# A mixture-of-experts kernel: products of the two widest experts split in three, a cast moved to ScalarE, and the order of h's halves changed

## The chip, the core and the metric

The kernel runs on one core of a Trainium2 chip, as one program. The metric is device time in microseconds; the kernel before takes 565.54 us (median of 3 runs, 563.86 to 566.18). The engines are named as in the profile: PE (TensorE) for matrix products, DVE (VectorE), ACT (ScalarE), POOL (GpSimd), and SP, whose queue issues most transfers. Times of the trace are us from the start of the span.

## What is computed

Attention with a threshold, then a layer that sends each of 1152 tokens to one of eight experts, then a SwiGLU layer, all in float32. The part that matters here is the middle one:

```python
logits = x @ w_gate                      # x: 1152 x 512, 8 experts
expert_idx = np.argmax(logits, axis=1)
# token i goes into its expert's rows, at most `capacity` (288) of them
h = np.maximum(np.einsum('ecd,edf->ecf', disp, w1), 0.0)   # 512 -> 1024
y = np.einsum('ecf,efd->ecd', h, w2)                       # 1024 -> 512
out[i] = gate_w[i] * y[expert_idx[i], pos[i]]
# and behind it
silu(out @ w_gate2) * (out @ w_val) @ w_out                # 512 -> 1536 -> 512
```

## The kernel before

**Precision.** Every operand of a product is kept as two parts, a rounded one (hi) and the rest (lo), and a product is made as hi x hi + hi x lo + lo x hi. What the text calls a *split* is the making of the two: a cast gives hi, a subtraction gives lo.

**Stages.** Attention is followed by a router that sorts the tokens by expert and the experts by how many tokens they have. `rest` then runs the experts in order of rank, fewest tokens first, with a fixed width of token columns for each rank: the list `FAST` (L56) is 128, 128, 128, 144, 176, 192, 224, 224. Other lists stand in two other branches, which don't run with these inputs. Ranks 0 to 2 run in another form (`expert_rows`). Ranks 3 to 7 run in `expert`, on which the change bears. In the trace rank 3 begins at 232.47 us, rank 4 at 249.81, rank 5 at 269.13, rank 6 at 288.73 and rank 7 at 309.68; the gate products (L1471, then L1460) begin at 332.02.

**One expert of width W.** Its token columns are taken out of `xsT` by `window` (L1219): DVE casts them into the hi half of `xw` (L1226) and subtracts for the lo half (L1227). That is done for rank e+1 just behind the first tile of rank e's second product (for rank 3 inside `expert_rows` of rank 2). The *first product* makes h in eight steps f = 0 to 7, each into a tile `ps_h` of PSUM: per step four pairs of matmuls, one of hi weights with hi and lo columns side by side (2W columns, L1231) and one of lo weights with the hi columns (W columns, L1232). The two column halves of the result are then added by `total` (L1236): ACT copies one half into `a` (L1240), DVE adds the other (L1241, the *sum*). `finish` (L1356) makes the split of h: ACT applies relu (L1357, hi), DVE makes the *remainder* (L1358, lo). `finish` of step f-1 is called at step f, after `total` of f. The *second product* makes y in four tiles m = 0 to 3, each over all eight h, with eight pairs; `total` adds the halves, ACT casts into `yT` (L1405) and DVE subtracts (L1406).

**Weights.** They come as raw pieces of 1 MB by DMA from SP's queue. Each piece is split by ACT (cast, L210) and DVE (L288). `next_piece` issues ACT's cast at once and keeps DVE's subtraction back until it is called the next time. In the first product it is called after every odd step, in the second after every tile. In rank 7 `pump` puts the decoding of the gate weights (64-bit values to float32, L231 to L238, on ACT and DVE) between the steps.

**Order.** In this part PE, ACT, DVE and POOL run in the order in which the code is written, each engine through its own queue. Nothing is reordered: an operation that waits holds up all behind it on its engine.

Of the kernel before, what the change touches and what calls it, by code (L numbers as in the profile page):

```python
# [22 lines left out]
def attention_moe_swiglu_kernel(  # L23
# [15 lines left out]
    nc = tc.nc  # L39
    B, H, S, D = q.shape  # L40
    NT, DM = out.shape
# [200 lines left out]
    def enqueue(it):  # L242
        while late:
            late.pop()()
        for x in range(NCV):
            if (it, x) not in converted:
                converted.add((it, x))
                queue.extend((it, op) for op in convert_ops(it, x))

    def pump(n=1):  # L250
        for _ in range(min(n, len(queue))):
            queue.popleft()[1]()
# [715 lines left out]
    V = nc.vector  # L968
# [53 lines left out]
    with nc.allow_low_precision("counts of at most 9 are exact in bfloat16"):  # L1022
        V.tensor_reduce(out=osb[:, 0:B],
                        in_=oh[:, 0:B * C4].rearrange("p (b t) e -> p b e t", b=B),
# [110 lines left out]
    def rest(ctx, WS, drops):  # L1135
# [33 lines left out]
        xsT = mx.tile([128, KD, YW], F32, name="xsT")  # L1169
# [3 lines left out]
        offs_v, offs_a = {0: 0}, {0: 0}  # L1173
# [5 lines left out]
        def sort_scale(t):  # L1179
            if t < NTL:  # L1180
                V.tensor_scalar(out=grow[t][:, 0:DM], in0=grow[t][:, 0:DM],
                                scalar1=grow[t][:, DM:DM + 1], scalar2=None, op0=ALU.mult)
# [14 lines left out]
        def mm3(o, wp, ws, x, xs, first, last):  # L1197
            mm(o, ws(wp, 0), xs(x, 0), start=first, stop=False)
            mm(o, ws(wp, 0), xs(x, 1), start=False, stop=False)
            mm(o, ws(wp, 1), xs(x, 0), start=False, stop=last)  # L1200
# [13 lines left out]
            ev()  # L1214
        sort_scale(NS0)
        sort_scale(NS0 + 1)
        V.memset(xsT[:, :, NT:], 0.0)

        def window(e):  # L1219
            offs_v[e] = ldv(e, EDVE)  # L1220
            offs_a[e] = ldv(e, EACT)
            xw = xws[e] = mw.tile([128, KD, 2 * WIN], F32R, tag="xw", name="xw")
            W = WS[e]
            assert steps["t"] * 128 >= (NT if drops else min(NT, sum(WS[:e + 1])))
            src = xsT[:, :, bass.ds(offs_v[e], W)]
            V.tensor_copy(out=xw[:, :, 0:W], in_=src)  # L1226
            V.tensor_tensor(out=xw[:, :, W:2 * W], in0=src, in1=f32(xw[:, :, 0:W]), op=ALU.subtract)  # L1227

        def mm_win(W, ps, wp, ws, x, first, last):
            if 2 * W <= 512:  # L1230
                mm(ps[:, 0:2 * W], ws(wp, 0), x[:, 0:2 * W], start=first, stop=False)  # L1231
                mm(ps[:, 0:W], ws(wp, 1), x[:, 0:W], start=False, stop=last)  # L1232
            else:
                mm3(ps[:, 0:W], wp, ws, x, lambda x, i: x[:, i * W:(i + 1) * W], first, last)

        def total(W, ps):  # L1236
            if 2 * W > 512:
                return ps[:, 0:W]
            a = sm.tile([128, WIN], F32, tag="a", name="a")[:, 0:W]
            nc.scalar.copy(a, ps[:, W:2 * W])  # L1240
            V.tensor_tensor(out=a, in0=a, in1=ps[:, 0:W], op=ALU.add)  # L1241
            return a
# [3 lines left out]
        def sort_step():  # L1246
            n, t = steps["n"], steps["t"]
            steps["n"] += 1
            for _ in range(1 if drops else SORT[n] if n < len(SORT) else 0):
                if t < NTL:  # L1250
                    sort_tile(t)()
                    sort_scale(t + 2)
                    if t == NG0 - 1:
                        idle.append(gbuf)
                        next_raw()
                    t += 1
            steps["t"] = t
# [86 lines left out]
        def flush_tail():  # L1344
            while tails:
                f, a = tails.pop()
                f(*a)

        def expert(e):
            if e < NE - 1 and WS[e] == 128:  # L1350
                return expert_rows(e)
            xw = xws.pop(e)
            W = WS[e]
            hs = []

            def finish(h, a):  # L1356
                nc.scalar.activation(out=h[:, 0:W], in_=a, func=ACTF.Relu)  # L1357
                V.scalar_tensor_tensor(out=h[:, W:2 * W], in0=a, scalar=0.0, in1=f32(h[:, 0:W]),  # L1358
                                       op0=ALU.max, op1=ALU.subtract)

            for f in range(KF):
                if f % 2 == 0:
                    wp = pieces.pop(("w1", e, f // 2))
                wv = wp[:, :, :].rearrange("p i (k f) -> p i k f", k=KD)
                ps = ps8.tile([128, 512], F32, tag="m", name="ps_h")
                fo = (f % 2) * 128
                for kk in range(KD):
                    mm_win(W, ps, wv, lambda w, i: w[:, i, kk, fo:fo + 128], xw[:, kk],
                           kk == 0, kk == KD - 1)
                flush_tail()  # L1370
                h = hp_.tile([128, 2 * WIN], F32R, tag="h", name="h")
                a = total(W, ps)
                if f:
                    finish(*prev)
                prev = h, a
                if f == KF - 1:
                    finish(*prev)
                hs.append(h)
                sort_step()
                if e == NE - 1:  # L1380
                    if f == CV:
                        enqueue(porder[npm])
                    pump(PU[f])
                for _ in range((EP if e and WS[e] < EW else (0, 1, 0, 1, 0, 1, 0, 1))[f]):
                    if used["piece"] < npm:
                        next_piece()
            for m in range(KD):
                ps = ps8.tile([128, 512], F32, tag="m", name="ps_y")
                if e in halves:
                    for f in range(KF):  # L1390
                        wv = pieces["w2", e, f // KD * 2 + m // 2][:, :, :].rearrange(
                            "p i (k f) -> p i k f", k=KD)
                        mm_win(W, ps, wv, lambda w, i: w[:, i, f % KD, m % 2 * 128:m % 2 * 128 + 128],
                               hs[f], f == 0, f == KF - 1)
                else:
                    wp = pieces.pop(("w2", e, m))
                    wv = wp[:, :, :].rearrange("p i (k f) -> p i k f", k=KF)
                    for f in range(KF):
                        mm_win(W, ps, wv, lambda w, i: w[:, i, f], hs[f], f == 0, f == KF - 1)
                if e == 0:  # L1400
                    sl_a = sl_v = slice(0, W)
                else:
                    sl_a, sl_v = bass.ds(offs_a[e], W), bass.ds(offs_v[e], W)
                a = total(W, ps)
                nc.scalar.copy(yT[:, 0, m, sl_a], a)  # L1405
                V.tensor_tensor(out=yT[:, 1, m, sl_v], in0=a, in1=f32(yT[:, 0, m, sl_v]),  # L1406
                                op=ALU.subtract)
                if e in halves and e < NE - 1:
                    for _ in range((0, 1, 0, 3)[m]):
                        next_piece()  # L1410
                elif e < NE - 1:
                    next_piece()
                else:
                    if m == MG[0]:
                        next_piece()
                    if m == MG[1]:
                        enqueue(porder[npm + 1])
                    pump(PU[KF + m])
                    if m == KD - 1:
                        next_piece()  # L1420
                if m == 0 and e + 1 < NE:
                    window(e + 1)

        for e in range(NE):
            expert(e)
            if e == SE:
                nc.scalar.activation(out=warm, in_=warm, func=ACTF.Silu)
# [89 lines left out]
    with tc.If(nmx <= NT, preferred_fallthrough_block=True) as cmp:  # L1517
        with ExitStack() as arm:
            rest(arm, FAST, False)
    with cmp.Else():  # L1520
        nmw = nc.values_load(slack[0:1, 1:2], min_val=0, max_val=2 * NT)
        with tc.If(nmw <= NT) as cmw:
            with ExitStack() as arm:
                rest(arm, WIDE, False)
        with cmw.Else():
            with ExitStack() as arm:
                rest(arm, SAFE, True)
# [29 lines left out]
```

## Time and profile before

| | |
|---|---|
| median of 3 runs | 565.54 us (563.86 to 566.18) |
| profiled execution | 564.97 us, its span 563.3 us |
| mean granted clock of PE | 0.986 |
| PE busy | 536.4 us (95% of the span) |
| DVE busy | 409.7 us (73%) |
| ACT busy | 295.2 us (52%) |
| POOL busy | 85.4 us (15%) |
| ranks 3 to 7 | 232.47 to 332.02 us |

The profile's page gives busy time for the whole span; the tables of stretches give it for one part. "Busy" of PE is a modelled time, since matmuls are pipelined: how long a matmul really takes of PE is read from the distance between the starts of two. An operation on DVE or ACT starts a little before the one in front ends. In a row of the timeline the bracket at the end is the idle time of the engine before that operation, and what ended it.

### The profile page before, as it was taken

What the parts mean: (1) busy time and instruction counts of PE and PEld (TensorE: products, weight loads), DVE (VectorE), ACT (ScalarE), POOL (GpSimd) and SP (SyncE); (2) the same over time, 40 slices, a digit from 0 to 9 for tenths busy, and PEclk for the clock granted to TensorE, in tenths of its full rate; (3) what the DMA queues carried; (4) which work ended last, traced back from release to release, by engine and by line L of the source; (5) the groups of instructions that cost most, each with busy time, mean ns of one, the idle gap of its engine ahead of it and who ended that gap; (6) DMA issues with size and microseconds to landing.
All of it is one profiled execution on the core that took longest, in us unless ns stands there. A gap on an engine that the chain in (4) does not pass through costs nothing. (4 is left out here: it accounts for less than half of the span.)

```text
span 563.3 us, 9844 instructions
## 1 busy us (share of the span) xinstructions
PE 536.4 (95%) x3600; PEld 481.0 (85%) x3602; DVE 409.7 (73%) x825; ACT 295.2 (52%) x573; POOL 85.4 (15%) x145
## 2 busy tenths in 40 slices
PE   7999988999997799999999999999999999999996
PEld 6787866877773799998998889999999999888884
DVE  5988876888876399989988977888896748722220
ACT  4977664676651399877866743334332333332321
POOL 6541050055452500000000000000000000011101
PEclk8999998999999799999999999999999999999999
DMA  7557467457301888977666442442341300000001
GB/s 185 173 150 171 118 143 172 110 140 205 116 29 35 313 289 281 328 224 232 224 219 223 151 149 81 145 149 83 143 149 76 112 40 1 0 38 37 20 38 42
DMA packets 67895, 77.94 MB, mean 138 GB/s; under 512 B 25216, under 2 KB 43136, under 8 KB 67840
## 3 DMA queue, kind: packets, MB, share of 16 engines
q1 hardware_dynamic: 66256, 72.52, 42.4%
q0 software_dynamic: 1440, 4.72, 2.2%
q8 instruction: 30, 0.49, 0.3%
q14 instruction: 25, 0.20, 0.1%
q10 hardware_dynamic: 144, 0.00, 0.0%
HBM read 61.89 MB, written 4.72 MB: 118 GB/s over the span
## 5 line engine op out<-in xcount | busy, mean ns | idle before, releaser
L1460 PE MATMUL pgv<-yT,ring 128*128 128x384 f32 x828 | 145.1, 337 | 0.0
L1460 PEld LDWEIGHTS pgv<-yT,ring 128*128 128x128 f32 x828 | 144.9, 188 | 0.0
L210 ACT CAST ring<-raw 128x1024 fp32r<-128x1024 f32 x57 | 60.8, 1066 | 51.2 <-DVE raw L238 49.5
L657 ACT COPY pT<-ps_pt 128x512 f32<-128x512 f32 (+1 forms) x108 | 52.3, 486 | 41.6 <-PE ps_pt L653 41.6
L607 DVE TENSOR_REDUCE nm<-s 128x1 f32<-128x576 f32 x72 | 54.4, 755 | 17.2 <-PE s L597 17.1
L631 DVE SCALAR_TENSOR_TENSOR e<-s,th,e 128x576 f32<-128x576 f32 x72 | 58.7, 816 | 6.2 <-ACT e L620 4.9
L1513 POOL DMA_INDIRECT out_dram<-ob,ids x9 | 8.7, 972 | 358.9 <-ACT ob L1512 351.7
L620 ACT ACTIVATE e<-s,nm 128x576 f32<-128x576 f32 x72 | 54.3, 754 | 2.2 <-DVE nm L607 1.8
L288 DVE TENSOR_TENSOR ring<-raw,ring 128x1024 fp32r<-128x1024 f32 x44 | 53.3, 1218 | 0.0
L1231 PE MATMUL ps_y<-h,ring 128*128 128x448 f32 (+3 forms) x160 | 48.8, 370 | 3.6 <-DVE h L1358 3.4
L214 DVE TENSOR_TENSOR hs<-h,hs 128x768 fp32r<-128x768 f32 x18 | 17.2, 958 | 48.1 <-ACT hs L210 48.1
L653 PE MATMUL ps_pt<-ident,e 128*128 128x128 f32 x324 | 47.9, 276 | 0.0
L1231 PE MATMUL ps_h<-xw,ring 128*128 128x448 f32 (+3 forms) x160 | 46.4, 362 | 0.0
L1508 PE MATMUL po<-ring,hs 128*128 128x512 f32 x108 | 42.0, 389 | 0.0
L1507 PE MATMUL po<-ring,hs 128*128 128x512 f32 x108 | 42.0, 389 | 0.0
L1509 PE MATMUL po<-ring,hs 128*128 128x512 f32 x108 | 42.0, 389 | 0.0
L1232 PE MATMUL ps_y<-h,ring 128*128 128x224 f32 (+3 forms) x160 | 40.0, 250 | 0.0
L1232 PE MATMUL ps_h<-xw,ring 128*128 128x224 f32 (+3 forms) x160 | 40.0, 250 | 0.0
L675 PE MATMUL ps_pv<-pT,v 128*64 128x256 f32 (+2 forms) x400 | 39.9, 331 | 0.0
L653 PEld LDWEIGHTS ps_pt<-ident,e 128*128 128x128 f32 x324 | 39.7, 142 | 0.2 <-issue 0.2
L1231 PEld LDWEIGHTS ps_y<-h,ring 128*128 128x128 f32 x160 | 30.0, 188 | 8.3 <-DVE h L1358 7.4
L1480 ACT ACTIVATE sg<-pgv 128x384 f32<-128x384 f32 x36 | 17.5, 486 | 28.4 <-PE pgv L1460 18.9
(224 smaller groups left out, 975.9 us busy)
## 6 DMA issues: line engine op xcount, KB each, us to landing
raw<-in_moe_w_dram SPq DMA_DIRECT2D x25, 1024.0 KB, 5.1
rawx<-in_moe_w_dram SPq DMA_DIRECT2D x7, 1024.0 KB, 5.9
raw<-in_moe_w_gate_dram SPq DMA_DIRECT2D x6, 1024.0 KB, 5.0
qhl<-ring SPq DMA_DIRECT2D x16, 256.0 KB, 4.4
raw<-in_moe_w_out_dram SPq DMA_DIRECT2D x4, 1024.0 KB, 4.9
kp<-ring SPq DMA_DIRECT2D x24, 128.0 KB, 2.3
rawx<-in_moe_w_val_dram SPq DMA_DIRECT2D x3, 1024.0 KB, 5.0
raw<-in_moe_w_val_dram SPq DMA_DIRECT2D x3, 1024.0 KB, 5.0
```

Of the source, the lines that this page charges most:

```text
L210: nc.scalar.copy(dst, src)
L288: lo_eng.tensor_tensor(out=lo_, in0=src, in1=f32(hi_), op=ALU.subtract)
L607: nc.vector.tensor_reduce(out=nm_t[u][:, j:j + 1], in_=s_t[i][:, :, 0:SH], axis=AX.XY, op=ALU.max, negate=True)
L620: nc.scalar.activation(out=e_t[u][:, j].rearrange("p (a s) -> p a s", a=2), in_=s_t[i][:, :, 0:SH], func=ACTF.Exp, bias=nm_t[u][:, j:j + 1 ...
L631: nc.vector.scalar_tensor_tensor(out=ev, in0=s_t.pop(i)[:, :, 0:SH], scalar=th_t[u][:, j:j + 1], in1=ev, op0=ALU.is_ge, op1=ALU.mult, accu ...
L653: nc.tensor.transpose(ps[:, c * 128:(c + 1) * 128], ef[:, (c0 + c) * 128:(c0 + c + 1) * 128], ident)
L657: return lambda: nc.scalar.copy(pT[g][:, c0:c0 + m, o:o + 128], ps[:, 0:m * 128].rearrange("p (c t) -> p c t", c=m))
L1231: mm(ps[:, 0:2 * W], ws(wp, 0), x[:, 0:2 * W], start=first, stop=False)
L1232: mm(ps[:, 0:W], ws(wp, 1), x[:, 0:W], start=False, stop=last)
L1460: mm(ps[:, 0:TH], (gw, vw)[w][:, i, kk, fl * 128:(fl + 1) * 128], yT[:, x, kk, th * TH:(th + 1) * TH], start=i + x + kk == 0, stop=i == 1 ...
L1507: mm(po, hs[:, 0, fl], ws[:, 0, sl], start=f == 0, stop=False)
L1508: mm(po, hs[:, 0, fl], ws[:, 1, sl], start=False, stop=False)
```

## The change

Four edits, all in `rest`: the clearing of the end of `xsT` goes from DVE to POOL; for widths over 128 the hi half of the window is made by ACT; the limit up to which two column halves lie side by side falls from 512 to 400 columns, so that width 224 (448 columns) takes the form that was there for wider ones, three matmuls of W columns into one tile, with nothing to add (`total` then returns the PSUM tile itself); and at step f `finish` of f-1 is called before `total` of f.

```diff
-        V.memset(xsT[:, :, NT:], 0.0)
+        nc.gpsimd.memset(xsT[:, :, NT:], 0.0)
...
-            V.tensor_copy(out=xw[:, :, 0:W], in_=src)
+            if W > 128:
+                nc.scalar.copy(xw[:, :, 0:W], xsT[:, :, bass.ds(offs_a[e], W)])
+            else:
+                V.tensor_copy(out=xw[:, :, 0:W], in_=src)
             V.tensor_tensor(out=xw[:, :, W:2 * W], in0=src, in1=f32(xw[:, :, 0:W]), op=ALU.subtract)
...
         def mm_win(W, ps, wp, ws, x, first, last):
-            if 2 * W <= 512:
+            if 2 * W <= 400:
                 mm(ps[:, 0:2 * W], ws(wp, 0), x[:, 0:2 * W], start=first, stop=False)
                 mm(ps[:, 0:W], ws(wp, 1), x[:, 0:W], start=False, stop=last)
             else:
                 mm3(ps[:, 0:W], wp, ws, x, lambda x, i: x[:, i * W:(i + 1) * W], first, last)
...
         def total(W, ps):
-            if 2 * W > 512:
+            if 2 * W > 400:
                 return ps[:, 0:W]
...
                 h = hp_.tile([128, 2 * WIN], F32R, tag="h", name="h")
-                a = total(W, ps)
                 if f:
                     finish(*prev)
+                a = total(W, ps)
                 prev = h, a
```

The form with three (`mm3`, L1197) is not new:

```python
        def mm3(o, wp, ws, x, xs, first, last):
            mm(o, ws(wp, 0), xs(x, 0), start=first, stop=False)
            mm(o, ws(wp, 0), xs(x, 1), start=False, stop=False)
            mm(o, ws(wp, 1), xs(x, 0), start=False, stop=last)
```

Lines of the kernel after are numbered three higher from `mm_win` on: the copy of `total` is L1243 there, the sum L1244, relu L1360, the remainder L1361, the subtraction of the window L1230, and ACT's cast of the window L1227.

DVE's queue at the last two steps of rank 4 (width 176), from the piece split behind step 5 to the one behind step 7. `a_...` is the tile of a step's sum, `h_...` that of its h. Before:

```order
L288 TENSOR_TENSOR ring0_95<-raw2_103,ring0_95 128x1024
L1241 TENSOR_TENSOR a_3673<-a_3673,ps_h_3663 128x176
L1358 SCALAR_TENSOR_TENSOR h_3654<-a_3655,h_3654 128x176
L1241 TENSOR_TENSOR a_3688<-a_3688,ps_h_3678 128x176
L1358 SCALAR_TENSOR_TENSOR h_3672<-a_3673,h_3672 128x176
L1358 SCALAR_TENSOR_TENSOR h_3687<-a_3688,h_3687 128x176
L288 TENSOR_TENSOR ring1_96<-raw1_102,ring1_96 128x1024
```

After:

```order
L288 TENSOR_TENSOR ring0_95<-raw2_103,ring0_95 128x1024
L1361 SCALAR_TENSOR_TENSOR h_3654<-a_3657,h_3654 128x176
L1244 TENSOR_TENSOR a_3675<-a_3675,ps_h_3663 128x176
L1361 SCALAR_TENSOR_TENSOR h_3672<-a_3675,h_3672 128x176
L1244 TENSOR_TENSOR a_3690<-a_3690,ps_h_3678 128x176
L1361 SCALAR_TENSOR_TENSOR h_3687<-a_3690,h_3687 128x176
L288 TENSOR_TENSOR ring1_96<-raw1_102,ring1_96 128x1024
```

The remainder of step 6 (h_3672) stood behind the sum of step 7 and now stands directly behind the sum of its own step (a_3675).

ACT's queue at the same place, up to the copy of the second product's first tile. Before:

```order
L210 CAST ring1_96<-raw1_102 128x1024
L1240 COPY a_3673<-ps_h_3663 128x176
L1357 ACTIVATE h_3654<-a_3655 128x176
L1240 COPY a_3688<-ps_h_3678 128x176
L1357 ACTIVATE h_3672<-a_3673 128x176
L1357 ACTIVATE h_3687<-a_3688 128x176
L210 CAST ring2_97<-raw1_102 128x1024
L1240 COPY a_3714<-ps_y_3697 128x176
```

After:

```order
L210 CAST ring1_96<-raw1_102 128x1024
L1360 ACTIVATE h_3654<-a_3657 128x176
L1243 COPY a_3675<-ps_h_3663 128x176
L1360 ACTIVATE h_3672<-a_3675 128x176
L1243 COPY a_3690<-ps_h_3678 128x176
L1360 ACTIVATE h_3687<-a_3690 128x176
L210 CAST ring2_97<-raw1_102 128x1024
L1243 COPY a_3714<-ps_y_3697 128x176
```

relu of a step, which needs that step's sum from DVE, now stands ahead of the next step's copy.

DVE's queue at the end of the first product of rank 7 (width 224) and its second product's first tile. L232 to L238 decode gate weights. Before:

```order
L1358 SCALAR_TENSOR_TENSOR h_4433<-a_4434,h_4433 128x224
L234 TENSOR_SCALAR wt_2626<-raw1_102 128x512
L1241 TENSOR_TENSOR a_4466<-a_4466,ps_h_4456 128x224
L1358 SCALAR_TENSOR_TENSOR h_4449<-a_4450,h_4449 128x224
L1358 SCALAR_TENSOR_TENSOR h_4465<-a_4466,h_4465 128x224
L236 SCALAR_TENSOR_TENSOR wt_2626<-raw1_102,wt_2626 128x512
L238 SCALAR_TENSOR_TENSOR raw1_102<-raw1_102,wt_2626 128x512
L1241 TENSOR_TENSOR a_4492<-a_4492,ps_y_4475 128x224
L1406 ISA
L1406 TENSOR_TENSOR yT_2662<-a_4492,yT_2662 128x224
```

After:

```order
L1361 SCALAR_TENSOR_TENSOR h_4470<-ps_h_4457,h_4470 128x224
L234 TENSOR_SCALAR wt_2626<-raw1_102 128x512
L1361 SCALAR_TENSOR_TENSOR h_4487<-ps_h_4474,h_4487 128x224
L1361 SCALAR_TENSOR_TENSOR h_4504<-ps_h_4491,h_4504 128x224
L236 SCALAR_TENSOR_TENSOR wt_2626<-raw1_102,wt_2626 128x512
L238 SCALAR_TENSOR_TENSOR raw1_102<-raw1_102,wt_2626 128x512
L1409 ISA
L1409 TENSOR_TENSOR yT_2662<-ps_y_4511,yT_2662 128x224
```

The sums (L1241) are gone, and the remainders read the products in PSUM (`ps_h_...`).

## Rows read from the trace of the kernel before

**Rows 1.** Page, part 1: busy us (share of the span) xinstructions.

```profile
PE 536.4 (95%) x3600; PEld 481.0 (85%) x3602; DVE 409.7 (73%) x825; ACT 295.2 (52%) x573; POOL 85.4 (15%) x145
```

**Rows 2.** Stretches of ranks 4, 7: length, busy PE, PEld, DVE, ACT, POOL (xinstructions), clock.

```profile
249.81:269.13 19.32, 18.20 (x131) 17.58 (x129) 17.38 (x36) 13.95 (x32) 0.00 (x0) 1.00 0.70 233
...
309.68:332.02 22.34, 21.32 (x130) 19.14 (x129) 20.58 (x41) 14.22 (x33) 0.00 (x0) 1.00 0.44 141
```

**Rows 3.** Timeline of PE, rank 4's second product: start us, us, instruction, [idle <-releaser].

```profile
261.22 0.43 PE L1231 MATMUL ps_y<-h,ring 128*128 128x352 f32 x1 [1.11 <-DVE h L1358]
```

**Rows 4.** Timeline of DVE, end of rank 4's first product.

```profile
257.30 1.22 DVE L288 TENSOR_TENSOR ring<-raw,ring 128x1024 fp32r<-128x1024 f32 x1
...
259.44 1.22 DVE L288 TENSOR_TENSOR ring<-raw,ring 128x1024 fp32r<-128x1024 f32 x1
...
260.83 0.33 DVE L1358 SCALAR_TENSOR_TENSOR h<-a,h 128x176 fp32r<-128x176 f32 x1
261.08 0.33 DVE L1241 TENSOR_TENSOR a<-a,ps_h 128x176 f32<-128x176 f32 x1
...
261.82 0.34 DVE L1358 SCALAR_TENSOR_TENSOR h<-a,h 128x176 fp32r<-128x176 f32 x1 [0.16 <-ACT h L1357]
```

**Rows 5.** Timelines of ACT and DVE where rank 5's window is made.

```profile
263.83 1.04 ACT L210 CAST ring<-rawx 128x1024 fp32r<-128x1024 f32 x1
...
265.36 0.55 DVE L1226 CAST xw<-xsT 128x768 fp32r x1
```

**Rows 6.** Groups by form, 229 to 340 us: xcount | busy us, mean ns | idle.

```profile
L1241 DVE TENSOR_TENSOR a<-a,ps_h 128x192 f32<-128x192 f32 x8 | 2.7, 348 | 0.0
...
L1241 DVE TENSOR_TENSOR a<-a,ps_h 128x144 f32<-128x144 f32 x8 | 2.3, 297 | 0.0
...
L1357 ACT ACTIVATE h<-a 128x192 fp32r<-128x192 f32 x8 | 2.9, 364 | 1.2 <-DVE a L1241 1.2
L1357 ACT ACTIVATE h<-a 128x176 fp32r<-128x176 f32 x8 | 2.8, 350 | 1.2 <-DVE a L1241 1.2
...
L1357 ACT ACTIVATE h<-a 128x144 fp32r<-128x144 f32 x8 | 2.6, 323 | 2.0 <-DVE a L1241 1.9
```

**Rows 7.** Stretches, PE alone: first products of ranks 4, 6 (32 pairs); L1460.

```profile
249.81:258.57 8.76, 8.76 (x66) 1.00 0.66 210
...
288.73:298.77 10.04, 10.04 (x66) 1.00 0.55 198
...
340.50:480.50 140.00, 140.00 (x802) 1.00 0.29 98
```

**Rows 8.** Timeline of PE: a product of `expert_rows`, what follows it, rank 6's last.

```profile
200.50 1.68 PE L1267 MATMUL ps_y<-ring,ht 128*128 128x256 f32 x12
202.03 0.60 PE L1187 MATMUL ps_g<-ident,g 128*128 128x128 f32 x4
...
298.67 0.26 PE L1232 MATMUL ps_h<-xw,ring 128*128 128x224 f32 x1
```

**Rows 9.** Timeline of PE: second products of ranks 6, 7, starts of tiles 0, 1.

```profile
298.77 0.38 PE L1231 MATMUL ps_y<-h,ring 128*128 128x448 f32 x1
...
302.16 0.37 PE L1231 MATMUL ps_y<-h,ring 128*128 128x448 f32 x1
...
319.71 0.37 PE L1231 MATMUL ps_y<-h,ring 128*128 128x448 f32 x1
...
324.50 0.38 PE L1231 MATMUL ps_y<-h,ring 128*128 128x448 f32 x1
```

**Rows 10.** Groups by form, PE: the first gate products.

```profile
L1471 PE MATMUL pgv<-yT,ring 128*128 128x384 f32 x36 | 7.5, 349 | 0.2 <-ACT yT L1405 0.2
```

**Rows 11.** Busy time by stretch, 84 to 92 us (attention).

```profile
84.00:92.00 8.00, 5.86 (x33) 4.37 (x34) 3.41 (x8) 2.78 (x6) 0.99 (x1) 0.79 0.68 154
```

**Rows 12.** Timeline of DVE where rank 0 begins.

```profile
191.04 0.81 DVE L1217 MEMSET xsT<- 128x896 f32 x1
...
196.36 0.69 DVE L1282 TENSOR_TENSOR ht<-ps_ht,ht 128x512 fp32r<-128x512 f32 x1 [3.10 <-ACT ht L1281]
```

## The prediction

> **What bounds the kernel now.** I read the page first, then a table of busy time by stretch, then the instructions of VectorE (DVE) and ScalarE (ACT) in time, expert by expert. On the page TensorE (PE) is busy 95% of the span [rows 1], so anything that only relieves another engine should be worth nothing. The stretches of the wide experts (ranks 3 to 7, widths 144, 176, 192, 224, 224) say otherwise: in rank 4's stretch DVE is busy for 17.38 of 19.32 us and PE for 18.20, and in rank 7's DVE for 20.58 of 22.34 [rows 2]. The place where they meet is the start of each second product: PE needs h of all eight steps there and sits idle for 1.11 us until L1358 on DVE delivers one [rows 3].
>
> DVE's own instructions show why. In rank 4 it runs without a gap: the low half of a weight piece (L288), sum, remainder, sum, remainder, and the next L288 begins 2.14 us after the one before (257.30, 259.44) [rows 4]. Two narrow operations follow each other at 0.25 us (260.83, 261.08), which is less than one lasts, since the next begins about 0.08 before the end. The exception is the last remainder: from the start of the sum at 261.08 to the start of the remainder that needs it at 261.82 are 0.74 us, because in between ACT has to make relu of the sum: 0.33 and a relu of 0.35 [rows 6] leave 0.06 for two hand-overs. So a sum, its relu on the other engine and its remainder are a **round trip** of 0.74 us, and the old order hides it behind the other step's operation everywhere but at the end.
>
> **The change, part by part.** The sum is made against the profiled run, 564.97 us (span 563.3); the median of the three runs shown is 0.57 above it.
>
> (a) *finish ahead of total*, widths 144, 176 and 192. At step f the remainder of step f-1 now stands in front of the sum of f, and so directly behind the sum of f-1; only after odd steps does an L288 lie between them. For every even step the round trip is therefore open: DVE waits for ACT, and all that is queued behind, the next sum and the next L288, waits with it. One open trip costs 0.74 - 0.25 = 0.49. Of the four pairs of steps the first pays half (today it already waits a little for its first relu), the two in the middle one each, and the last one and a half (its two trips stand one behind the other, where today a remainder fills half of the one): four in all, 1.97 us for width 176. For 144, with a mean sum of 0.297, a mean relu of 0.323 and 0.06 for the two hand-overs, a trip is 0.68 and the hidden spacing 0.22, so 4 x 0.46 = 1.84; for 192 it is 0.77 and 0.27, so 4 x 0.50 = 2.00 [rows 6]. DVE has no gap to take this from, and PE already waits for exactly this chain, so I put it on the path in full: **+5.8 us**. If DVE had slack there, it would be 0; that is the low end.
>
> (b) *Columns rounded on ACT.* DVE loses a cast: 0.55 us from 265.36, and a hand-over of 0.03 to its reader. In its place the subtraction waits for ACT. ACT's piece cast before it ends at 263.83 + 1.04 = 264.87 [rows 5]; a cast of 768 columns, between the 364 ns of 192 columns [rows 6] and the 1.04 us of 1024 [rows 5], comes to about 0.83, so it ends near 265.65, and the subtraction begins some 0.29 earlier than today. What is queued behind it on ACT is the copy of the next second product, which DVE can't use before the subtraction is over. Of the five windows those for ranks 4 and 5 lie in the stretch that DVE bounds: **-0.6 us**. The one for rank 3 starts in a stretch where ACT is just as full (0 taken, 0.4 at most); those for ranks 6 and 7 lie before stretches that PE bounds afterwards (0).
>
> (c) *Three narrow products* for width 224: 128 times (two experts, 32 in each product) 448 and 224 columns become three of 224. From the table of counted matmuls a pair takes 10.04/32 = 0.314 us at 448+224 and 8.76/32 = 0.274 at 352+176, and a long run of 384 columns 140.0/802 = 0.175, which is 0.160 of columns at 2.4 GHz and 0.015 [rows 7]. Take 0.015 and the columns of the wide product off the pairs and 0.112 is left for the narrow one, at 224 columns and at 176 alike: it does not follow its columns (0.093 and 0.073). I read this as the exchange of weights that every product needs and a narrow one doesn't cover. Three of them are 0.336, 0.022 more than the pair: **+2.8 us**. The bounds: 0.10 from a 224's start to the next product's start (298.67 and 298.77 [rows 8, 9]) gives 0.30 and -1.8; a run of twelve 256-column products, (202.03 - 200.50)/12 = 0.128 [rows 8], gives 0.383 and +8.8. I take 0.112, since it comes from the same tiles. The Trainium skill, "TensorE: Matmul & The Clock Gate", has a rule on each side: under "LDWEIGHTS (loading the stationary operand)" a load takes its columns over 1.2, 107 ns for 128, by which the triple would be an estimated 0.320 and this term +0.8; under "Back-to-back issue gap" it gives N/2.4 + 2.5 ns, 96 for 224, by which it would be 0.288 and -3.4. The trace's 0.112 in the pairs agrees with the first and not with the second.
>
> (d) *No sum at width 224.* ACT loses 24 copies and DVE 24 sums, and the round trip is not closed by a sum any more: relu and remainder read the products where they are. Rank 7's 20.58 us of DVE lose 12 sums at some 0.3, leaving 17, while PE's part grows to 64 x 0.336 = 21.5, so DVE falls behind no longer; the last remainder comes under a microsecond after the last first product, and the second product asks for it after seven triples, 2.35 us. The waits at the start of the second product go: rank 6's first tile takes 302.16 - 298.77 = 3.39 where eight pairs are 2.51, rank 7's 324.50 - 319.71 = 4.79 [rows 9]: 0.88 + 2.28, **-3.2 us**.
>
> (e) *Start of the gate products.* L1471 is busy 7.5 us and waits 0.2 for 36 products that take 6.3 at the spacing of [rows 7] and 0.2 for the last to end [rows 10]: 1.2 us lost to yT, whose copy and sum stand in a full DVE queue. With neither, and DVE back in time, ACT casts the last tile at once and 18 products (3.1 us) lie ahead of its reader: **-1.2 us**; 0 if the conversions still delay it.
>
> (f) *memset on GpSimd.* DVE is rid of 0.81 us, but waits 3.10 for ACT soon after [rows 12]: nothing. On GpSimd it stands behind the last gather; its readers, the windows, come after that wait. Without this cover it costs about its own length.
>
> Sum: 5.8 - 0.6 + 2.8 - 3.2 - 1.2 = +3.6, so 568.6 against the profiled run and 569.1 against the median. I give **569.1**.
>
> **Rivals.** *Narrow products cost their columns.* If the 0.112 belongs to the change of width in the pair and not to a reload, the triple takes three times 0.10, (c) is -1.8, and the whole 564.97 - 1.0, so 564.0 to 564.5 by the two bases: not slower. For it speaks the spacing of 0.10 that the trace shows; against it that the pair as a whole doesn't add up so. It decides from a triple of 0.308 downwards. Chance 0.15. The gap rule of the Trainium skill cited in (c) would act the same way and give an estimated 562.4 against the profiled run.
>
> *DVE hides the round trip.* If PE were the bound at ranks 3 to 5, each finish would be done while PE computes the next step; (a) is 0 and the rest stands: -2.2, about 563. Should the earlier remainders also shorten the waits of ranks 3 to 5, some 561. It decides from a slack of half a microsecond per pair of steps on DVE; the gapless queue speaks against it. Chance 0.10.
>
> *The clock falls.* With (a) PE waits some 3 us at the start of the second product of ranks 3 to 5. In the stretch from 84 to 92 us PE is busy 5.86 of 8 with its waits at the front, and its granted clock averages 0.79 [rows 11]: it went down to 1.2 GHz and back. At ranks 3 and 4 DVE's lag would hide a slower PE; after rank 5 PE is the bound, and a fall as long as that one takes 0.21 x 8 = 1.7 us: about 570.5. Chance 0.15.
>
> **How the numbers follow.** My forecast has 0.60 and reaches from 567.5 to 570.5 by its smaller terms. Below it are the narrow rival (to 564) and the hidden round trip (to 561), above it the clock and part of the upper bound of (c), so the range is 565.2 to 572.6. Within 0.5%, about what a measurement of this kernel can tell, is 562.7 to 568.4. Slower: three quarters of the forecast, all of the clock's share, 0.61; within: a quarter of the forecast, most of the narrow rival, part of the hidden trip, 0.31; faster: what is left of these two, 0.08.
>
> **What would show it.** After the change DVE in ranks 3 to 5 must show idle time before remainders, ended by relu on ACT, about half a microsecond each, and L288 at 2.6 us instead of 2.14 at width 176; PE's wait at the start of their second products grows by nearly 2 us each. Ranks 6 and 7 must show no such wait, and 32 triples 10.75 us instead of 10.04. L1471 shouldn't wait. If the remainders don't wait for ACT, (a) is wrong and the kernel is no slower; if the triple is near 0.30, (c) is.

## The result, and the profile after

The kernel after takes **569.33 us** (median of 10 runs, 566.96 to 572.53), the kernel before beside it on the same chip 565.58 us (10 runs, 563.86 to 566.91). The ratio on record is 1.0082, with a 95% interval of 1.0059 to 1.0106: slower by 3.3 to 6.0 us. (The two medians by themselves give 1.0066.) The profiled execution took 568.68 us, 3.7 more than the profiled one of before.

PE's share is the same 95% as in [rows 1], and DVE and ACT are a little less busy. The page as a whole tells nothing of the loss.

```profile
PE 539.6 (95%) x3730; PEld 488.5 (86%) x3730; DVE 404.2 (71%) x795; ACT 292.2 (52%) x554; POOL 86.4 (15%) x146
```

The stretches of ranks 3 to 7, in the columns of [rows 2] (length, busy PE, PEld, DVE, ACT, POOL, clock, DMA):

```profile
232.17:252.38 20.21, 18.23 (x134) 17.63 (x132) 16.81 (x35) 14.47 (x35) 0.00 (x0) 0.92 0.79 262
252.38:273.63 21.25, 19.79 (x130) 19.15 (x129) 17.04 (x34) 15.04 (x34) 0.00 (x0) 0.92 0.60 199
273.63:293.98 20.35, 19.16 (x131) 18.46 (x129) 16.55 (x32) 13.99 (x33) 0.00 (x0) 1.00 0.61 196
293.98:315.43 21.45, 21.45 (x195) 21.45 (x193) 16.03 (x24) 13.78 (x24) 0.00 (x0) 1.00 0.63 208
315.43:336.87 21.44, 21.44 (x195) 21.44 (x193) 18.11 (x32) 10.24 (x20) 0.00 (x0) 1.00 0.52 173
```

By the starts given in the text on the kernel before, these stretches took 17.34, 19.32, 19.60, 20.95 and 22.34 us. So ranks 3, 4 and 5 lose 2.9, 1.9 and 0.75 us, rank 6 loses 0.5, and rank 7 gains 0.9. In ranks 6 and 7 PE now has no idle time at all (21.45 of 21.45). In rank 4 DVE is less busy than in [rows 2] (17.04 against 17.38) in a stretch that is 1.9 us longer. That the clock's mean is 0.92 in ranks 3 and 4 comes up again below.

DVE at the end of rank 4's first product, the place of [rows 4] (start us, us, instruction, and in brackets the idle time before it and what ended it; L1244 is the sum, L1361 the remainder):

```profile
258.97 1.22 DVE L288 TENSOR_TENSOR ring<-raw,ring 128x1024 fp32r<-128x1024 f32 x1
260.10 0.33 DVE L1361 SCALAR_TENSOR_TENSOR h<-a,h 128x176 fp32r<-128x176 f32 x1
260.35 0.33 DVE L1244 TENSOR_TENSOR a<-a,ps_h 128x176 f32<-128x176 f32 x1
261.10 0.34 DVE L1361 SCALAR_TENSOR_TENSOR h<-a,h 128x176 fp32r<-128x176 f32 x1 [0.42 <-ACT h L1360]
261.36 0.33 DVE L1244 TENSOR_TENSOR a<-a,ps_h 128x176 f32<-128x176 f32 x1
261.61 1.22 DVE L288 TENSOR_TENSOR ring<-raw,ring 128x1024 fp32r<-128x1024 f32 x1
...
263.00 0.33 DVE L1244 TENSOR_TENSOR a<-a,ps_h 128x176 f32<-128x176 f32 x1
263.74 0.34 DVE L1361 SCALAR_TENSOR_TENSOR h<-a,h 128x176 fp32r<-128x176 f32 x1 [0.42 <-ACT h L1360]
264.00 0.33 DVE L1244 TENSOR_TENSOR a<-a,ps_h 128x176 f32<-128x176 f32 x1
264.75 0.34 DVE L1361 SCALAR_TENSOR_TENSOR h<-a,h 128x176 fp32r<-128x176 f32 x1 [0.42 <-ACT h L1360]
```

The queue that had no gap now has one in front of every second remainder (and of the last one too), ended by relu on ACT. From a sum's start to its remainder's are 0.74 us (263.00, 263.74), and the L288 follow each other at 2.64 us (258.97, 261.61) instead of 2.14. In the same pairs ACT waits for the sum ahead of each such relu:

```profile
260.72 0.35 ACT L1360 ACTIVATE h<-a 128x176 fp32r<-128x176 f32 x1 [0.70 <-DVE a L1244]
...
263.36 0.35 ACT L1360 ACTIVATE h<-a 128x176 fp32r<-128x176 f32 x1 [0.71 <-DVE a L1244]
```

So the two engines wait for each other in turn, and neither is at its limit. The group of all remainders by width, with their idle time behind the last bar:

```profile
L1361 DVE SCALAR_TENSOR_TENSOR h<-a,h 128x192 fp32r<-128x192 f32 x8 | 2.9, 356 | 2.1 <-ACT h L1360 2.1
...
L1361 DVE SCALAR_TENSOR_TENSOR h<-a,h 128x176 fp32r<-128x176 f32 x8 | 2.7, 340 | 2.1 <-ACT h L1360 2.1
...
L1361 DVE SCALAR_TENSOR_TENSOR h<-a,h 128x144 fp32r<-128x144 f32 x8 | 2.4, 306 | 1.9 <-ACT h L1360 1.9
```

Before, the same group at width 176 was idle for 0.3 us:

```profile
L1358 DVE SCALAR_TENSOR_TENSOR h<-a,h 128x176 fp32r<-128x176 f32 x8 | 2.7, 340 | 0.3 <-ACT h L1357 0.3
```

So DVE waits 1.6 to 1.8 us more in each of the three ranks. Each wait also loses the 0.08 by which an operation otherwise starts before the one in front ends, and with that the loss is some 2 us per rank.

### The profile page after: what moved, and what is told of

Its sections match the earlier page's. It is cut to its first block, busy times and chain, and to the rows that moved or that the text cites. A ratio compares the mean times of both kernels' runs of the same rounds, so it can differ in the third digit from the quotient of the medians.

```text
span 567.0 us, 10043 instructions
## 1 busy us (share of the span) xinstructions
PE 539.6 (95%) x3730; PEld 488.5 (86%) x3730; DVE 404.2 (71%) x795; ACT 292.2 (52%) x554; POOL 86.4 (15%) x146
## 5 line engine op out<-in xcount | busy, mean ns | idle before, releaser
L288 DVE TENSOR_TENSOR ring<-raw,ring 128x1024 fp32r<-128x1024 f32 x44 | 53.2, 1218 | 0.0
L1234 PE MATMUL ps_y<-h,ring 128*128 128x288 f32 (+2 forms) x96 | 30.7, 389 | 4.6 <-DVE h L1361 4.5
L1484 DVE TENSOR_TENSOR h<-sg,pgv 128x384 f32<-128x384 f32 x36 | 19.7, 549 | 18.9 <-PE pgv L1463 18.6
L675 PEld LDWEIGHTS ps_pv<-pT,v 128*64 128x64 f32 x400 | 21.4, 136 | 12.3 <-issue 3.2
L597 PE MATMUL s<-kp,ring 128*128 128x288 f32 x128 | 26.5, 328 | 5.7 <-DMA kp<-thl 2.9
L210 ACT CAST ring<-rawx 128x1024 fp32r<-128x1024 f32 x19 | 20.1, 1068 | 20.2 <-DVE rawx L238 20.2
```

The lines of the kernel that those rows point to most:

```text
L210: nc.scalar.copy(dst, src)
L288: lo_eng.tensor_tensor(out=lo_, in0=src, in1=f32(hi_), op=ALU.subtract)
L675: mm(ps[j * D:(j + 1) * D, o:o + w], r["v"][:, bb, j, c, :], p[:, j * (C4 + 1) + c, o:o + w], start=c == 0, stop=False)
```

## The experiments

All are compared with a run of the kernel before on their own chip: 566.03 us (11 runs) for the first four, 564.75 us (23 runs) for the last four. Since attention, whose code is the same, ends up to 3 us earlier or later from one profile to the next (rank 3 begins between 230.80 and 234.06), the traces are also compared from rank 3's start to the end of the span: 330.8 us before (563.3 - 232.47) and 334.8 after (567.0 - 232.17).

**The order undone.** The kernel after, with `total` ahead of `finish` again.

```diff
+                a = total(W, ps)
                 if f:
                     finish(*prev)
-                a = total(W, ps)
```

> The changed kernel with total ahead of finish again; its other edits stay. Theory (open round trips on DVE at ranks 3 to 5 cost 5.8 us): it gets them back, 569.3 - 5.8 = 563.5, that is 2 us under the kernel before; L288 at width 176 every 2.14 us again instead of 2.65, no remainder that waits half a microsecond for relu. Rival (the loss comes from the three narrow products, or from the columns rounded on ACT): the order gives back little, 568 to 569.5.

561.40 us, ratio 0.9933 (0.9912 to 0.9953). From rank 3 on 328.2 us. The stretches of ranks 3 to 5 are 16.85, 19.02 and 19.31 us long, against 20.21, 21.25 and 20.35 above, and those of ranks 6 and 7 are the same as after. Rank 4's, in the columns used above:

```profile
247.65:266.67 19.02, 18.19 (x130) 17.56 (x129) 16.77 (x35) 14.68 (x34) 0.00 (x0) 1.00 0.69 233
```

The whole loss lies in the order, and what is left of the change is a gain. From rank 3 on the traces give back 6.6 us, where 5.8 was expected: the rest fits the clock, which doesn't fall in this part without the longer waits (0.75 us, below). The medians differ by more, 7.9 us; what of that lies ahead of rank 3 the traces don't settle.

**The order alone.** The kernel before, with nothing but this swap.

```diff
-                a = total(W, ps)
                 if f:
                     finish(*prev)
+                a = total(W, ps)
```

> The kernel before with only the order of finish and total exchanged. Theory: 5.9 us at ranks 3 to 5, and as width 224 still has its sums, 4 x (0.83 - 0.30) = 2.1 at rank 6 and up to as much at rank 7, where decoding of gate weights lies between some steps and fills a part: 565.6 + 8 to 10 = 573.5 to 575.5. Rival (the order is worth nothing, or helps, as remainders are made earlier): 564 to 566.

576.82 us, ratio 1.0174 (1.0144 to 1.0204), and from rank 3 on 341.1 us: 10.3 more than before, somewhat more than expected. Here width 224 still has a sum, so all five ranks have the round trip; the stretches grow by 4.1, 1.9, 0.7, 2.2 and 1.3 us. From a rank's first sum to its last remainder DVE takes 9.4 us longer in the five ranks together, which is inside the 8 to 10 expected; the other 0.9 is time that DVE lost behind ranks 3 and 4, where the clock fell, as in the kernel after (below).

**A finish of two steps back.** The remainder still stands ahead of the sum, on DVE and on ACT, but it is that of step f-2.

```diff
-                if f:
-                    finish(*prev)
+                if f > 1:
+                    finish(*prev.pop(0))
                 a = total(W, ps)
-                prev = h, a
+                prev = (prev if f else []) + [(h, a)]
                 if f == KF - 1:
-                    finish(*prev)
+                    for p in prev:
+                        finish(*p)
```

> The changed kernel, finish still ahead of total, but of the step before the last (f-2 instead of f-1), the last two behind the loop. relu still stands ahead of the next copy on ACT, but a remainder no longer stands behind its own sum. Theory (round trip): closed again by the other step's operations, so as with the old order, 563.5. Rival (what costs is that the copy waits behind relu on ACT, or that finish comes first as such): no gain, 569.3.

561.28 us, ratio 0.9911 (0.9889 to 0.9932), and from rank 3 on 327.4 us. Its DVE in rank 4:

```profile
258.48 1.22 DVE L288 TENSOR_TENSOR ring<-raw,ring 128x1024 fp32r<-128x1024 f32 x1
259.62 0.34 DVE L1361 SCALAR_TENSOR_TENSOR h<-a,h 128x176 fp32r<-128x176 f32 x1
259.87 0.33 DVE L1244 TENSOR_TENSOR a<-a,ps_h 128x176 f32<-128x176 f32 x1
260.12 0.34 DVE L1361 SCALAR_TENSOR_TENSOR h<-a,h 128x176 fp32r<-128x176 f32 x1
```

Remainder ahead of sum costs nothing here, where that remainder's relu was made a step ago: the sequence is that of the kernel after, without its gaps. So it isn't the place of the remainder that costs, but that it follows its own sum with nothing between. This kernel is faster than before and after; with the one of the old order it can't be told apart by its time.

**DVE's order alone.** The kernel after; ACT runs in the old order (copy of f, then relu of f-1), DVE in the new one.

```diff
-                if f:
-                    finish(*prev)
-                a = total(W, ps)
+                a = total(W, ps, (lambda: finish(*prev)) if f else lambda: None)
...
-        def total(W, ps):
+        def total(W, ps, between=lambda: None):
...
             nc.scalar.copy(a, ps[:, W:2 * W])
+            between()
```

> The changed kernel with ACT's queue as before the change (copy of f, then relu of f-1) and only DVE's as after it (remainder of f-1, then sum of f). Theory: the remainder still stands directly behind its own sum, so the trip is as open as in the changed kernel: 569.3, L288 at width 176 every 2.65 us. Rival (the cost is ACT's order, a copy held up by a relu that waits for DVE): about 563.5.

569.11 us, ratio 1.0061 (1.0040 to 1.0082), from rank 3 on 334.8 us, as after. Its DVE in rank 4 (L1365 is the remainder, L1362 relu) has the same waits and the same 2.64 us from one L288 to the next:

```profile
259.06 1.22 DVE L288 TENSOR_TENSOR ring<-raw,ring 128x1024 fp32r<-128x1024 f32 x1
...
261.19 0.34 DVE L1365 SCALAR_TENSOR_TENSOR h<-a,h 128x176 fp32r<-128x176 f32 x1 [0.42 <-ACT h L1362]
...
261.70 1.22 DVE L288 TENSOR_TENSOR ring<-raw,ring 128x1024 fp32r<-128x1024 f32 x1
```

ACT's order adds nothing to the loss once DVE's has made it.

**ACT's order alone.** The other half: ACT in the new order (relu of f-1, then copy of f), DVE in the old one (sum of f, then remainder of f-1). `relu` and `rem` are the two halves of `finish`, ACT's and DVE's.

```diff
                 if f:
-                    finish(*prev)
+                    relu(*prev)
                 a = total(W, ps)
+                if f:
+                    rem(*prev)
```

> The kernel after with DVE's old order (sum of step f, then remainder of step f-1), but ACT's new one (relu of f-1, then copy of f). If what costs time is that DVE has nothing to do while a sum goes through relu, this closes another round trip: sum of f-1, relu of f-1 on ACT, copy of f on ACT, sum of f, about 0.4 us or more open per pair of steps, so 1.2 to 2 us per rank for ranks 3 to 5 and about 565 to 567. If only the place of the remainder on DVE matters, the time is that of the kernel with the old order on both engines, 561.4.

569.84 us, ratio 1.0100 (1.0061 to 1.0140), from rank 3 on 334.9 us. This is as slow as the kernel after, with another ring. DVE in its rank 4 (L1246 is the sum here, L1365 the remainder, L1244 the copy on ACT):

```profile
261.47 0.34 DVE L1246 TENSOR_TENSOR a<-a,ps_h 128x176 f32<-128x176 f32 x1 [0.36 <-ACT a L1244]
...
261.98 1.22 DVE L288 TENSOR_TENSOR ring<-raw,ring 128x1024 fp32r<-128x1024 f32 x1
263.12 0.33 DVE L1246 TENSOR_TENSOR a<-a,ps_h 128x176 f32<-128x176 f32 x1
...
264.06 0.34 DVE L1246 TENSOR_TENSOR a<-a,ps_h 128x176 f32<-128x176 f32 x1 [0.36 <-ACT a L1244]
...
264.56 1.22 DVE L288 TENSOR_TENSOR ring<-raw,ring 128x1024 fp32r<-128x1024 f32 x1
```

Now the sum waits, for a copy that stands on ACT behind a relu that needs the previous sum. Its period, 2.58 us (261.98, 264.56), is that of the kernel after less 0.06. The rival, that only the remainder's place on DVE matters, is out. The 565 to 567 that were expected were too low all the same. The ring has the size expected: from the first sum to the last remainder DVE takes 1.6, 1.8 and 1.9 us more than with the order undone. But the clock was at 1.2 GHz for 6.8 us in rank 3's second product, and behind that rank DVE lost another 1.4 us (12.03 from its last remainder to the next rank's first sum, against 10.59).

**The narrow products alone.** The kernel before, with the limit of 400 in `mm_win` and `total`.

```diff
-            if 2 * W <= 512:
+            if 2 * W <= 400:
...
-            if 2 * W > 512:
+            if 2 * W > 400:
```

> The kernel before with one edit: width 224 in three narrow products without a sum (the limit 400 instead of 512). The theory of the prediction gives (c) +2.8, (d) -3.2, (e) -1.2, so -1.6 us, about 564.0 where the kernel before is at 565.6; the stages of ranks 6 and 7 in the trace of the kernel after (21.45 and 21.44 us against 20.95 and 22.34, the gate products' stretch 0.96 shorter) give -1.4, the same within what can be told. The rival, that the narrow products are the reason why the kernel after is slower, gives more than 566.

563.36 us, ratio 0.9969 (0.9941 to 0.9997); from rank 3 on 329.2 us, 1.6 less than before. A small gain, as expected, though 32 triples of each product take longer than the pairs did (rank 6's first product, columns as above; in [rows 7] it has 10.04):

```profile
288.88:299.61 10.73, 10.73 (x98) 10.73 (x97) 9.10 (x16) 7.84 (x15) 0.00 (x0) 1.00 0.69 224
```

**The window alone.** The kernel before, with ACT's cast in `window`.

```diff
-            V.tensor_copy(out=xw[:, :, 0:W], in_=src)
+            if W > 128:
+                nc.scalar.copy(xw[:, :, 0:W], xsT[:, :, bass.ds(offs_a[e], W)])
+            else:
+                V.tensor_copy(out=xw[:, :, 0:W], in_=src)
```

> The kernel before with one edit: the hi half of the window made by ACT for widths over 128. By the prediction -0.6 us (ranks 4 and 5 only), 565.0; with rank 3's window, which gained some 0.5 us in the trace of the kernel after, and those of ranks 6 and 7, whose second products still wait for DVE here, up to -1.6 us, 564.0. A rival, that ACT is late with what is queued behind its cast, gives no gain or more than 565.6.

563.60 us, ratio 0.9988 (0.9965 to 1.0012): by time this settles nothing. By the trace it is 329.1 us from rank 3 on, 1.7 less than before, and regular: the stretches of ranks 3 to 7 are shorter by 0.50, 0.30, 0.31, 0.29 and 0.32 us. Rank 5's window in this kernel, the hi half on ACT and the lo half on DVE:

```profile
L1230 DVE TENSOR_TENSOR xw<-xsT,xw 128x768 fp32r<-128x768 f32 x1 | 1.0, 959 | 0.2 <-ACT xw L1227 0.2
...
L1227 ACT CAST xw<-xsT 128x768 fp32r x1 | 0.8, 830 | 0.0
```

The subtraction waits 0.2 for ACT, where DVE's own cast had taken 0.55 [rows 5]. At rank 3's window it waits for nothing; it begins 0.79 us after the remainder in front of it, 1.28 before (228.84 and 230.12 there):

```profile
227.28 0.69 DVE L1285 TENSOR_TENSOR ht<-ps_ht,ht 128x512 fp32r<-128x512 f32 x1 [0.34 <-ACT ht L1284]
228.07 0.76 DVE L1230 TENSOR_TENSOR xw<-xsT,xw 128x576 fp32r<-128x576 f32 x1
```

**Half of the third product.** The kernel after, with the product of the lo weights cut to 112 columns.

```diff
-            mm(o, ws(wp, 1), xs(x, 0), start=False, stop=last)
+            n = 112 if WS is FAST else None
+            mm(o[:, 0:n], ws(wp, 1), xs(x, 0)[:, 0:n], start=False, stop=last)
```

> The kernel after, but the third narrow product of each triple (lo weights) is made for 112 columns only at width 224; it leaves out the other 112 columns of that term, so its outputs lack a small part there. If a narrow product costs the exchange of its weights, 32 triples of rank 6's first product still take about 10.7 us. If it costs its columns, 112 columns less at 2.4 GHz are 0.047 us each, and the 32 take 9.2 us.

One run, 570.95 us. The first product of its rank 6 takes 10.69 us, against 10.73 after, and this is how PE gets there (L1201 is the product with 112 columns):

```profile
296.24:306.93 10.69, 10.69 (x99) 10.69 (x97) 8.37 (x14) 6.89 (x14) 0.00 (x0) 1.00 0.63 209
```

```profile
304.25 0.33 PE L1198 MATMUL ps_h<-xw,ring 128*128 128x224 f32 x1
304.41 0.27 PE L1199 MATMUL ps_h<-xw,ring 128*128 128x224 f32 x1
304.52 0.22 PE L1201 MATMUL ps_h<-xw,ring 128*128 128x112 f32 x1
304.58 0.33 PE L1198 MATMUL ps_h<-xw,ring 128*128 128x224 f32 x1
304.74 0.27 PE L1199 MATMUL ps_h<-xw,ring 128*128 128x224 f32 x1
```

Behind the short product the next one starts after 0.06 (304.52, 304.58), and the one behind that after 0.16 instead of 0.11, so that a triple still takes 0.33. What the columns leave is given back at the next start. The loads of the weights at the same place, on their own row of the profile, show what sets the pace:

```profile
304.42 0.19 PEld L1201 LDWEIGHTS ps_h<-xw,ring 128*128 128x128 f32 x1
304.53 0.19 PEld L1198 LDWEIGHTS ps_h<-xw,ring 128*128 128x128 f32 x1
304.64 0.19 PEld L1199 LDWEIGHTS ps_h<-xw,ring 128*128 128x128 f32 x1
304.75 0.19 PEld L1201 LDWEIGHTS ps_h<-xw,ring 128*128 128x128 f32 x1
```

They start 0.11 apart throughout, whatever is multiplied with them, so here it is the loads and not the columns that a triple costs.

## Why the prediction was right

The prediction was 569.1 us with a sum of +3.6 against the profiled run; measured were 569.33 and +3.7 between the two profiles. Step by step:

**(a) The round trip: right in mechanism and size.** From the first sum of a rank to its last remainder DVE took 7.26, 7.67 and 7.90 us before (ranks 3 to 5) and 9.04, 9.68 and 9.99 after: +1.78, +2.01 and +2.09, together 5.9 where 1.84, 1.97 and 2.00 were reckoned. The one open trip is 0.74 against 0.25, as worked out. That DVE hides it (the second rival) is out.

One sign that was named for it was wrong. PE's wait at the start of the second product was to grow by nearly 2 us each; in rank 4 it is now in three pieces:

```profile
263.13 0.43 PE L1234 MATMUL ps_y<-h,ring 128*128 128x352 f32 x1 [0.47 <-DVE h L1361]
...
264.14 0.43 PE L1234 MATMUL ps_y<-h,ring 128*128 128x352 f32 x1 [0.50 <-DVE h L1361]
...
265.15 0.44 PE L1234 MATMUL ps_y<-h,ring 128*128 128x352 f32 x1 [0.49 <-DVE h L1361]
```

From the product's start at 261.14 to 265.15 are 4.0 us for seven pairs that need 0.274 each [rows 7], so 2.1 us of waiting; before, the same seven pairs waited 1.7 (258.57 to 262.22). The loss was there, but PE had spent most of it, 1.6 us, at a lower clock in rank 3's second product (below), and so came later to the same h. In rank 5 the same waiting grew by 0.7 us, for the same reason. In rank 3, ahead of any fall, it grew by 1.3: the 1.8 of (a) less the 0.5 that the window gave (next).

**(b) The window: right in sign, one part mis-sized.** ACT's cast of 768 columns was reckoned at 0.83 us and is 0.83. The windows for ranks 4 and 5 gave 0.3 each, as reckoned, and those for ranks 6 and 7 gain 0.3 each only as long as DVE bounds their ranks: with the narrow products the stretches are 21.45 and 21.44 us with the cast on ACT and without. The step that failed is rank 3's window, at which 0 was taken "in a stretch where ACT is just as full", 0.4 at most: it gave 0.5. With ACT's cast the subtraction follows the remainder in front of it at once, since the cast (0.68 us) was done meanwhile. So this term was -1.1, not -0.6.

**(c) The narrow products: right.** 32 triples take 10.73 us where 10.75 was reckoned, 0.69 more than the pairs; four such products are +2.8. Two in a row stand 0.11 apart in the kernel after, too:

```profile
326.15 0.27 PE L1198 MATMUL ps_y<-h,ring 128*128 128x224 f32 x1
326.26 0.28 PE L1199 MATMUL ps_y<-h,ring 128*128 128x224 f32 x1
326.37 0.28 PE L1200 MATMUL ps_y<-h,ring 128*128 128x224 f32 x1
```

The first rival needed a triple of 0.308 or less; it is 0.335. Of the two rules of the Trainium skill, "TensorE: Matmul & The Clock Gate", that stood there, the load's (section "LDWEIGHTS (loading the stationary operand)", 107 ns for 128 columns) is the one that the trace bears out, at 112. The gap's formula (section "Back-to-back issue gap", 96 ns) was taken too widely in the prediction: the section gives it for a product by itself, and says that in a stream of loads and products both set the spacing. The trace agrees with that: each product here has a load of its own, and the run with 112 columns shows the load's pace.

**(d) and (e): right.** Ranks 6 and 7 together take 42.89 us instead of 43.29; with +2.76 for the triples that is -3.2 for the waits, as reckoned. The rows just above are the start of rank 7's second product: it waits for nothing. DVE keeps 18.1 us of work in rank 7, not 17, without consequence. The gate products no longer wait (7.5 us busy and 0.2 idle in [rows 10]):

```profile
L1474 PE MATMUL pgv<-yT,ring 128*128 128x384 f32 x36 | 6.5, 337 | 0.0
```

From there to the last stage are 151.22 us instead of 152.38: -1.2.

**(f)** The memset runs on POOL from 192.84 on, for 0.86 us behind the last gather, and DVE still waits for ACT soon after it would have been done (1.01 us, at 196.12). From rank 0's first product to rank 3's start are 44.2 to 45.3 us in the profiles with the memset on DVE and 44.7 to 45.5 in those with it on POOL, so no gain or loss can be told from the variation; it wasn't tried by itself.

**The clock: a rival that came in part.** A stretch of the kernel after and, below it, one of the run with 112 columns (the granted clock is the number behind POOL's, 0.79 in both):

```profile
264.00:272.00 8.00, 7.37 (x41) 7.15 (x41) 6.28 (x11) 5.51 (x10) 0.00 (x0) 0.79 0.69 217
```

```profile
284.00:292.00 8.00, 5.82 (x27) 5.14 (x26) 6.43 (x11) 5.25 (x12) 0.00 (x0) 0.79 0.44 137
```

In the kernel after the clock went down to 1.2 GHz for 3.4 us at 245.8 and again at 266.3, in the second products of ranks 3 and 4, each time just after PE had waited there. Before and with the order undone it stays at 2.4 GHz throughout these ranks. The other profiles agree: the clock goes down in rank 3's second product in all five kernels in which the trip or the other ring is open, and in ranks 3 to 7 of the other five it doesn't. A fall costs PE some 1.6 us (1.59 more busy in rank 4's stretch than in [rows 2]), but, as the rival had it, DVE's lag hides most of it in these two ranks: from a last remainder to the next rank's first sum DVE lost 0.23 us behind rank 3 and 0.52 behind rank 4 (10.89 before, less 0.3 for the window, against 10.82; 11.40 less 0.3 against 11.62). The fall behind rank 5, which was to cost 1.7 us, is not in the profile of the kernel after. It is in the run with 112 columns, at 288.1 us, and there the time from rank 5's last remainder to rank 6's start is 9.20 us (287.04 to 296.24) against 7.62 (286.36 to 293.98): 1.6.

So the sum of the parts from rank 3 on is 5.9 - 1.1 + 2.8 - 3.2 - 1.2 + 0.75, that is +4.0, which is what the two traces differ by there; 0.3 came back because rank 3 began earlier, part of what varies from one profile to the next. Two errors of the prediction, 0.5 for the window and 0.75 for the clock, nearly cancelled, so that the total came out so close is partly luck; the parts themselves are not.

The kernel after also varies more (566.96 to 572.53) than the one before. Falls of the clock behind other ranks in other executions would do that, and the run with 112 columns shows one. Three of the four slowest executions (570.87, 572.09 and 572.53 us) have mean granted clocks of 0.978 to 0.982, the six fastest 0.981 to 0.988. But only one of the ten has a trace, so where the clock fell in the others stays open.

## What to carry to other kernels

Before moving an operation in the queue of an in-order engine, follow its inputs: if one comes from another engine that in turn needs the operation just in front, the move opens a round trip, and its price is the trip less the distance at which the two used to follow, times the number of trips left open (here it came to four in a rank of eight steps, since a weight piece fills every other one). It can be read from any place of the old trace where the pair already stands without cover, here the last step. Moving a use ahead was free here where its input was a whole step old, and a part of a change that gains is worth measuring without its neighbours: here the same change without the new order is 0.7% faster than the kernel before instead of 0.8% slower.

## What the runs showed of the hardware

Either half of the reordering alone made a kernel as slow as both: 0.36 us of waiting per pair of steps where ACT's queue was turned, 0.42 where DVE's was, and 0.42, not their sum, with both. A product with weights of its own took 0.11 us at 224 columns, and shortening it to 112 gave nothing to the triple, because the next one started that much later: the loads of the weights kept coming 0.11 apart. And where the new order made PE wait, its clock went down at places where it had stood at 2.4 GHz. A fall of 3.4 us cost 0.2 to 0.5 us where DVE was behind anyway and 1.6 where PE bounded what followed; the falls of 6.8 us in rank 3 of three other runs cost 0.7 to 1.4 us beside a DVE that was behind.
